# Attention with normalised q and k, then a SiLU feed-forward, on one Trainium2 core: every second product of w_in is summed in a score tile

## The chip, the core and the metric

The program runs on one core of one Trainium2 chip. A core has TensorE (matmuls, PE in the profile), VectorE (DVE), ScalarE (ACT), GpSimd (POOL) and SyncE (SP, which here only issues transfers). They run beside each other, each taking its own instructions in order, and wait for each other by semaphores. Matmuls write to PSUM, which has eight banks of 512 floats in each of 128 partitions; here VectorE and ScalarE read it. The metric is the device time of one execution in microseconds (us), lower is better.

## The reference

Attention for 8 batches of 12 heads, 448 rows, 64 columns each, and then a feed-forward part on the 3584 rows of 768 columns that come out:

```python
q_n, k_n = (rmsnorm(q, g_q), rmsnorm(k, g_k))
scores = scale * np.matmul(q_n, k_n.transpose(0, 1, 3, 2))
attn = softmax(scores)          # exp(scores - max) / (sum + 1e-9)
x = np.matmul(attn, v)          # then (B,H,S,D) -> (B*S, H*D)
h = x @ w_in                    # 768 x 2048
out = (h * (1.0 / (1.0 + np.exp(-h)))) @ w_out      # 2048 x 768
```

All is float32.

## The kernel before

**Attention in visits.** The 96 heads are worked in 24 visits (c = 0 to 23) of four heads. `visit(c)` issues the score matmuls (L712), the exps that empty them (L717, ScalarE), and the weighted sums over v (`weigh`, L749) of this visit and the end of the last one. The sums of the weights are added up on VectorE (`add`, L763). In `between(c)` the next visit's q and k are prepared and `sum_up` (L783) sums the weights over keys with matmuls; two reciprocals (L792, VectorE) read that result, and they are what `divide` needs in the next visit. Up to visit 10, q and k are transposed for the next visit by matmuls: `transpose_q` (L629, emptied by ScalarE, L633) before the first half of `between`, `transpose_k` (L647, emptied by ScalarE, L649) before its second half. From visit 11 on VectorE transposes instead (`flip`, L658), with no PSUM. The squares for the norms are taken by ScalarE and summed by VectorE (L467, L468).

**Products of w_in as filler.** The feed-forward part takes two batches (six visits) at a time. x @ w_in is done with Strassen's scheme in the form with seven products (class `Seven`): for each of eight blocks m of w_in, seven products of three matmul steps each (`HW` = 3), each step a 128x128 by 128x448 matmul. That makes 168 steps for two batches. They are put between the visits of the next six as filler: `fill` is called twice in each `between`, once for each half, and takes steps from the generator until what is due is used up. `filler["due"]` is counted in columns, and `S` = 448 columns are one step. A half holds 13 steps in visits 6 to 11 and 14 in visits 12 to 23 (two blocks of the first two batches are begun earlier, in visits 3 to 5, with 2.4 steps a half). The products of the last two batches come after the visits, in a stage of their own.

Beside the steps, `fill` deals out other work to the queues: the adds, the unpacking and sums of w_in (`weights_in`), the squares for later visits. `prompt` work, the reciprocals above all, is issued at the start of a half and after every third step. When a product has ended, the next thing its generator does is to issue the instruction that empties it: ScalarE's copy for products 1 and 5 (L907, L917), VectorE's add for the others (L857).

**PSUM.** Three pools share the eight banks during the visits. `ps_mm` holds two tiles "mm" of one bank: all products of w_in, and `sum_up` up to visit 4. In `ps`, the tile "sc" has two buffers of two banks each: scores, transposes, `sum_up` from visit 5 on, and one small product in `scale`. "av0" and "av1" take a bank each. After the visits `ps` is closed, and `ps_alone` holds six banks for what follows. A tile's buffer can be written again when all readers of its former tile are done; a matmul that begins the new tile waits for that. The function `bank` (L879) gives a product its place: a tile "mm" during the visits, later one of eight in turn.

The order of all instructions is written out by hand (`manual_schedule`); each engine follows the order of the calls.

Of the kernel before, what the change touches and what calls it, by code (L numbers as in the profile page):

```python
# [11 lines left out]
F32 = mybir.dt.float32  # L12
# [15 lines left out]
BANK = 512  # L28
# [162 lines left out]
def kernel(  # L191
# [246 lines left out]
    with tc.If(taken > 0) as cond:  # L438
        with tc.manual_schedule():
            bounded(**arm())  # L440
# [95 lines left out]
def bounded(  # L536
# [3 lines left out]
    P, D, R, J, S = z.P, z.D, z.R, z.J, z.S  # L540
# [5 lines left out]
    ps = others.enter_context(tc.tile_pool(name="ps", bufs=1, space=bass.MemoryType.PSUM))  # L546
# [14 lines left out]
    work = mem.tile([P, 16 * S + z.NK], F32, name="work")  # L561
# [22 lines left out]
    n = 2 * room.COLS  # L584
# [81 lines left out]
    n = z.NK // z.Q  # L666
# [100 lines left out]
    def sum_up(c):  # L767
# [4 lines left out]
        n = D // 2  # L772
        early = c < GROUP
        t = bank(S) if c < GROUP - 1 else ps.tile([P, 2, BANK], F32, name="sc", bufs=2)[:, 0, 0:S]
        terms = [(0, lambda: weights(c, 0))]
        if early:
# [97 lines left out]
        minus(b21, t2, t4)  # L874

    ps_alone = None
    turns = dict(next=0)

    def bank(n):  # L879
        turn = turns["next"] = (turns["next"] + 1) % 4  # L880
        if ps_alone is None or turn == 0:
            return ps_mm.tile([P, BANK], F32, name="mm")[:, 0:n]
        return ps_alone.tile([P, BANK], F32, name="alone")[:, 0:n]

    class Seven:
# [10 lines left out]
        def product(self, name):  # L896
            t, ends = bank(self.n), (self.steps[0], self.steps[-1])
            for s in self.steps:
                nc.tensor.matmul(  # L899
                    t, self.left(name, s), self.right(name, s), start=s == ends[0], stop=s == ends[1]  # L900
                )
                if not (self.prompt and s == ends[1]):
                    yield self.n
            return t
# [217 lines left out]
    aside = [a[:, ts(t, z.HALF)] for t in range(2)]  # L1122
# [72 lines left out]
    def deep(name, out, more, following, then=lambda t, h: None):  # L1195
# [6 lines left out]
        def product(of):  # L1202
            t = bank(QUARTER)
            for i in ORDER:
                x, y = of_seven(of, a, deep_right(name, i))
                nc.tensor.matmul(t, x[:, i], y, start=i == ORDER[0], stop=i == ORDER[-1])  # L1206
            return t
# [114 lines left out]
        fetch(q + 1, 0, 1)  # L1322


    filler = dict(work=iter(()), due=0.0, share=0.0)

    def begin(work, columns, parts):
        finish()
        filler.update(work=work, due=0.0, share=columns / parts)
# [197 lines left out]
    for c in range(NC):  # L1527
# [4 lines left out]
    ps_alone = ctx.enter_context(  # L1532
        tc.tile_pool(name="ps_alone", bufs=6, space=bass.MemoryType.PSUM)
    )
# [221 lines left out]
```

## Time and profile before

| | |
|---|---|
| Time, median of 3 runs | 1331.36 us (1330.54 to 1336.35) |
| The profiled execution's own time | 1330.28 us |
| Its span, first to last instruction | 1328.5 us |
| TensorE busy | 1298.6 us (98%) |
| VectorE, ScalarE, GpSimd busy | 949.4, 505.7, 362.0 us |
| Mean granted TensorE clock | 0.998 |

In this profile the first 133 us hold visits 0 to 5, the stretch from 133 to 746 us visits 6 to 23 with products of w_in between them, and the rest the last products of w_in and the products with w_out. A float32 matmul is done in two passes, so a step of a product is two rows of MATMUL and a product of three steps is six. Rows of the timeline give the start, the length from the first start to the last end of equal instructions that follow each other, engine, line, operation, the tiles written and read, and in square brackets the idle time before and what ended it. In the view of the waits a line reads: who waits, for whom, us in total, times, the longest.

### The profile page before, as it was taken

What the parts mean: (1) busy time and instruction counts of PE and PEld (TensorE: products, weight loads), DVE (VectorE), ACT (ScalarE), POOL (GpSimd) and SP (SyncE); (2) the same over time, 40 slices, a digit from 0 to 9 for tenths busy, and PEclk for the clock granted to TensorE, in tenths of its full rate; (3) what the DMA queues carried; (4) which work ended last, traced back from release to release, by engine and by line L of the source; (5) the groups of instructions that cost most, each with busy time, mean ns of one, the idle gap of its engine ahead of it and who ended that gap; (6) DMA issues with size and microseconds to landing.
All of it is one profiled execution on the core that took longest, in us unless ns stands there. A gap on an engine that the chain in (4) does not pass through costs nothing.

```text
span 1328.5 us, 19796 instructions
## 1 busy us (share of the span) xinstructions
PE 1298.6 (98%) x7193; PEld 829.5 (62%) x7193; DVE 949.4 (71%) x1629; ACT 505.7 (38%) x886; POOL 362.0 (27%) x230
## 2 busy tenths in 40 slices
PE   8998999999999999999999999999999999999998
PEld 4343444444444444344444455558999999999998
DVE  6888777775855555754554686688978787878785
ACT  7867566645455555455545244410000000001000
POOL 6766444353234333342330144410000000000000
PEclk9999999999999999999999999999999999999999
DMA  9665337234344444344421357512323232332311
GB/s 239 163 178 139 91 90 208 80 88 95 86 116 93 97 98 113 89 94 107 95 67 46 119 174 263 166 66 76 100 76 100 77 104 82 99 107 69 128 48 39
DMA packets 249439, 144.94 MB, mean 109 GB/s; under 512 B 184292, under 2 KB 233220, under 8 KB 249332
## 3 DMA queue, kind: packets, MB, share of 16 engines
q1 hardware_dynamic: 248672, 142.42, 38.2%
q8 instruction: 59, 0.97, 0.3%
q0 software_dynamic: 352, 0.96, 0.2%
q14 instruction: 48, 0.39, 0.1%
q10 hardware_dynamic: 308, 0.20, 0.1%
HBM read 93.98 MB, written 41.29 MB: 102 GB/s over the span
## 4 chain that ended last, share of the span: by engine, by line
PE 83%; DVE 7%; ACT 4%; issue 2%; DMA 2%; POOL 1%; SPq 0%; ACTq 0%; DVEq 0%; POOLq 0%
PE mm L899 24%; PE alone L1206 22%; PE av L749 8%; PE sc L712 8%; PE mm L1206 8%; PE alone L899 7%; PE alone L1243 2%; DVE work L763 2%; PE sc L783 1%; DVE sums_x L854 1%; PE mm L1243 1%; ACT stage L1037 1%; ACT work L717 1%; DMA rows<-in_v_dram 1%; ACT L1037 1%
## 5 line engine op out<-in xcount | busy, mean ns | idle before, releaser
L899 PE MATMUL mm<-x,W 128*128 128x448 f32 x612 | 246.6, 546 | 4.6 <-DVE parts L857 2.1
L717 ACT ACTIVATE work<-sc,rms 128x448 f32<-128x448 f32 x324 | 184.7, 633 | 67.4 <-PE sc L712 62.8
L899 PE MATMUL mm<-sums_x,W 128*128 128x448 f32 x480 | 195.9, 547 | 5.5 <-DVE stage L857 3.8
L899 PEld LDWEIGHTS mm<-x,W 128*128 128x128 f32 x612 | 112.3, 190 | 131.2 <-issue 104.7
L712 PE MATMUL sc<-work 64*64 64x448 f32 x1344 | 164.3, 543 | 1.8 <-ACT work L717 1.5
L763 DVE TENSOR_TENSOR work<-work 128x896 f32<-128x896 f32 (+1 forms) x114 | 123.8, 1117 | 53.5 <-PE av L749 52.9
L749 PE MATMUL av<-work,rows 64*64 64x448 f32 x1296 | 153.4, 541 | 4.1 <-DMA rows<-in_v_dram 2.0
L899 PEld LDWEIGHTS mm<-sums_x,W 128*128 128x128 f32 x480 | 90.1, 191 | 101.0 <-issue 86.0
L496 POOL TENSOR_TENSOR rms<-rms,minus_half 128x14 f32<-128x14 f32 (+4 forms) x43 | 106.3, 2474 | 158.9 <-DVE rms L492 149.4
L523 POOL DMA_DIRECT2D out_dram<-x x2 | 1.2, 594 | 443.3 <-DVE x L857 443.3
L1206 PE MATMUL alone<-W,rows 128*128 128x192 f32 x610 | 113.0, 326 | 0.0
L749 PEld LDWEIGHTS av<-work,rows 64*64 64x64 f32 x1296 | 57.9, 132 | 75.8 <-issue 35.2
L1206 PEld LDWEIGHTS alone<-W,rows 128*128 128x128 f32 x610 | 101.5, 190 | 0.0
L712 PEld LDWEIGHTS sc<-work 64*64 64x64 f32 x1344 | 53.4, 132 | 73.0 <-ACT work L717 27.9
L919 POOL TENSOR_TENSOR parts<-parts,stage 128x448 f32<-128x448 f32 x31 | 42.0, 1356 | 148.5 <-DVE parts L857 148.1
L688 POOL TENSOR_TENSOR rms<-rms,minus_half 128x28 f32<-128x28 f32 x12 | 57.5, 4794 | 61.3 <-DVE rms L685 61.3
L1206 PE MATMUL alone<-W,work 128*128 128x192 f32 x382 | 72.2, 326 | 0.0
L1037 ACT ACTIVATE stage<-stage 128x896 f32<-128x896 f32 x63 | 57.3, 945 | 23.3 <-DVE stage L857 22.5
L468 DVE TENSOR_REDUCE rms<-rows 128x8 f32<-128x512 f32 (+2 forms) x56 | 35.8, 640 | 40.3 <-ACT rows L467 38.8
L1216 ACT COPY rows<-alone 128x192 f32<-128x192 f32 x33 | 10.5, 318 | 142.1 <-PE alone L1206 78.4
L1206 PEld LDWEIGHTS alone<-W,work 128*128 128x128 f32 x382 | 63.8, 190 | 0.0
L792 DVE RECIPROCAL work<-sc 128x224 f32<-128x224 f32 x38 | 58.6, 1546 | 5.4 <-PE sc L783 5.2
(250 smaller groups left out, 2112.6 us busy)
## 6 DMA issues: line engine op xcount, KB each, us to landing
hidden<-stage SPq DMA_DIRECT2D x63, 448.0 KB, 3.1
work<-hidden SPq DMA_DIRECT2D x21, 1024.0 KB, 5.2
rows<-in_moe_w_out_dram SPq DMA_DIRECT2D x32, 384.0 KB, 3.6
W<-in_moe_w_in_dram SPq DMA_DIRECT2D x22, 512.0 KB, 5.4
work<-work SPq DMA_DIRECT2D x141, 56.0 KB, 2.0
x<-hidden SPq DMA_DIRECT2D x7, 1024.0 KB, 5.5
rows<-in_q_dram SPq DMA_DIRECT2D x96, 56.0 KB, 2.2
rows<-in_k_dram SPq DMA_DIRECT2D x96, 56.0 KB, 2.2
```

The lines of the kernel that those rows point to most:

```text
L496: nc.gpsimd.tensor_tensor(out=t, in0=t, in1=half, op=ALU.pow)
L688: nc.gpsimd.tensor_tensor(out=f, in0=f, in1=minus_half.to_broadcast([P, n]), op=ALU.pow)
L712: nc.tensor.matmul(two[ds(half * D, D), h, 0:S], keys[rows, ts(half, D)], qT[rows, pair, :], start=True, stop=True,)
L717: nc.scalar.activation(eleft[:, h] if j == LEFT else weights(c, j)[:, i, h], two[:, h, 0:S], AF.Exp, scale=norm.column(c, i, h, j),)
L749: nc.tensor.matmul(sums[i][ds(h * D, D), :], v, w, start=(j == 0 and step == 1), stop=(j == LEFT - 1 and step == 1),)
L763: nc.vector.tensor_tensor(out=total, in0=total, in1=more, op=ALU.add)
L792: nc.vector.reciprocal(out=r[0][:, rows], in_=t[:, rows])
L899: nc.tensor.matmul(t, self.left(name, s), self.right(name, s), start=s == ends[0], stop=s == ends[1])
L919: nc.gpsimd.tensor_tensor(out=u2, in0=u2, in1=p5, op=ALU.add)
L1037: nc.scalar.activation(t, t, AF.Silu)
L1206: nc.tensor.matmul(t, x[:, i], y, start=i == ORDER[0], stop=i == ORDER[-1])
L1243: nc.tensor.matmul(o, a[:, 2 * i + m, t], right_one(name, i)[:, m], start=n == 0, stop=n == len(steps) - 1,)
```

## The change

`bank` gets a second kind of place during the visits. When a product begins, more than five steps are still due in this half, and the product before it did not get such a place, it is summed in the first bank of a tile "sc" instead of a tile "mm". Otherwise it gets "mm" as before. `turns["aside"]` remembers which the last product had. The dictionary `filler` is defined earlier, since `bank` now reads it; outside `fill` its due is zero or below. Nothing else is changed: the same matmuls in the same order, emptied by the same instructions.

```diff
     ps_alone = None
-    turns = dict(next=0)
+    turns = dict(next=0, aside=False)
+    filler = dict(work=iter(()), due=0.0, share=0.0)
 
     def bank(n):
         turn = turns["next"] = (turns["next"] + 1) % 4
+        if ps_alone is None and filler["due"] > 5 * S and not turns["aside"]:
+            turns["aside"] = True
+            return ps.tile([P, 2, BANK], F32, name="sc", bufs=2)[:, 0, 0:n]
+        turns["aside"] = False
         if ps_alone is None or turn == 0:
             return ps_mm.tile([P, BANK], F32, name="mm")[:, 0:n]
         return ps_alone.tile([P, BANK], F32, name="alone")[:, 0:n]
...
-
-    filler = dict(work=iter(()), due=0.0, share=0.0)
```

## The prediction

> **What bounds the kernel now.** I read the busy shares and the chain first.
>
> ```profile
> PE 1298.6 (98%) x7193; PEld 829.5 (62%) x7193; DVE 949.4 (71%) x1629; ACT 505.7 (38%) x886; POOL 362.0 (27%) x230
> PE 83%; DVE 7%; ACT 4%; issue 2%; DMA 2%; POOL 1%; SPq 0%; ACTq 0%; DVEq 0%; POOLq 0%
> ```
>
> TensorE is the bound, so an edit that adds no work to it is worth what TensorE waits. The waits by pair come next (us in total, times, longest).
>
> ```profile
> PE mm L899 <- DVE stage L857: 5.4, 4, 1.9
> PE mm L899 <- DVE parts L857: 3.0, 6, 0.9
> PE mm L899 <- DVE sums_x L854: 0.6, 1, 0.6
> PE mm L899 <- ACT stage L917: 0.6, 1, 0.6
> ```
>
> Products of w_in (L899) wait 9.6 us in all for other engines, 9.0 us of it for instructions that empty an mm place. So the prize is small: under 1% of 1328.5 us. What one wait is like shows in the timeline of visit 12, when VectorE has a queue.
>
> ```profile
> 345.73 0.91 PE L899 MATMUL mm<-sums_x,W 128*128 128x448 f32 x2
> 348.55 1.40 PE L899 MATMUL mm<-sums_x,W 128*128 128x448 f32 x3 [1.91 <-DVE stage L857]
> ...
> 345.91 2.05 DVE L763 TENSOR_TENSOR work<-work 128x896 f32<-128x896 f32 x2
> 347.88 0.62 DVE L857 TENSOR_TENSOR stage<-mm,stage 128x448 f32<-128x448 f32 x1
> ```
>
> A pass is shown 0.54 long, but passes start 0.37 apart (two rows take 0.91), so a product of six passes takes 2.25 us. The last pass before the wait began at 0.91-0.54 after 345.73, 346.10; the next at 348.55, 2.45 later instead of 0.37. After the wait, three passes take 1.40: two spacings of 0.43 instead of 0.37. A wait thus costs its idle time plus 0.16 plus 0.10. Last, the granted clock (third figure from the end: 1.00, then 0.51) around the twin of this wait, in visit 18:
>
> ```profile
> 551.40:554.80 3.40, 1.52 (x5) 0.47 (x3) 3.40 (x5) 0.00 (x0) 0.00 (x0) 1.00 0.31 51
> 554.80:558.30 3.50, 3.50 (x5) 1.64 (x6) 3.16 (x4) 0.00 (x0) 0.00 (x0) 0.51 0.69 124
> ...
> 554.71 4.22 PE L899 MATMUL mm<-sums_x,W 128*128 128x448 f32 x6 [1.88 <-DVE stage L857]
> ```
>
> After 1.88 us idle the clock is halved for 3.4 us; six passes take 4.22 instead of 2.42.
>
> **What is removed.** In visits 6 to 23 a half holds 13 or 14 steps. By the rule "due over five steps", its first product of those with six to come goes to a score tile, the next to mm, the third again to a score tile if six are left: two per half, mostly. An mm place is then written again two products later than now in the middle of a half, so a product may be emptied some 2.3 us later without a wait. None of the waits above is much longer than that, so all for an mm place go.
> - Listed waits: 9.0, less 0.7 of the four "stage" waits (at 96 us, in visit 4, where no half holds six steps), is 8.3 us in ten waits; with 10 x 0.26 that is **10.9**. The 0.6 for sums_x is for data and stays.
> - Starts held up by 0.06 to 0.3 us, too short for that view (about a dozen in the spacing of the passes, some of them for data): by estimate **2.5** with their 0.10 each.
> - The halved clock: 4.22-2.42 = 1.8, less the 0.10 counted above: **1.7**.
> Removed: 15.1 us.
>
> **What is added.** No engine gets an instruction: same matmuls, same evacuations, other addresses. The moved definition of filler costs nothing. What comes is waits for score tiles, which have their own readers. In visits 6 to 10 the keys are transposed into one (L647) just before the second half, then sum_up takes the other, so the first product of the half falls on the tile of the keys, and waits for ScalarE's copy (L649). The profile has both rows, for visits 7 and 10:
>
> ```profile
> 177.87 0.93 PE L647 MATMUL sc<-ident,rows 128*128 128x128 f32 x7
> 179.61 2.52 PE L899 MATMUL mm<-sums_x,W 128*128 128x448 f32 x6
> ...
> 180.03 0.99 ACT L649 ACTIVATE work<-sc,gains 128x896 f32<-128x896 f32 x1
> ...
> 284.08 2.52 PE L899 MATMUL mm<-x,W 128*128 128x448 f32 x6
> ...
> 283.38 0.67 DVE L468 TENSOR_REDUCE rms<-rows 128x8 f32<-128x512 f32 x1
> ...
> 284.52 0.99 ACT L649 ACTIVATE work<-sc,gains 128x896 f32<-128x896 f32 x1
> ```
>
> The copy is late because ScalarE stands behind a square (L467) that waits for VectorE's sum (L468).
> - Visit 7: copy ends 181.02, product starts 179.61: 1.4 + 0.10. Visit 8: the copy (215.17, 0.99 long) ends 216.16, the product starts 214.68: 1.5 + 0.10.
> - Visit 10: 285.51 against 284.08, 1.4; but the 0.86 idle at 279.97 before it is gone, with its 0.26, and VectorE's row at 283.38 stands behind sums of weights without a gap, so it doesn't come earlier: 1.4 + 1.1 + 0.1 = 2.6.
> - Visits 6 and 9: the copies end at 146.49 and 250.03, the products start 147.87 and 250.37: nothing. In the first half of visit 9 the exps end 237.69, the product starts 237.23: 0.5 + 0.1.
> Together **6.4**. Behind a product that waits stand the whole half on TensorE and, on VectorE, only its own evacuation; the keys' copy is needed in the next visit alone.
> The third product of a second half takes the tile of sum_up, which two reciprocals read:
>
> ```profile
> 320.78 1.54 DVE L792 RECIPROCAL work<-sc 128x224 f32<-128x224 f32 x1
> ...
> 321.77 3.17 PE L899 MATMUL mm<-x,W 128*128 128x448 f32 x8
> ```
>
> The second ends at 322.32, the product starts as the fifth of these passes at 323.28: 0.95 spare, as in most visits from 11 on (0.5 to 2.2). I cost it at nothing; the slow rival lifts that cover. From both sides, the score waits cost 0 (the copies come as in visits 6 and 9) to 2.6 in each of five visits, 13; the three rows decide for 6.4.
>
> **What is late next.** In visit 12 TensorE arrives 2.2 us earlier, but VectorE does not: sum_up (352.51) needs an add that ends at 351.14, so of the new start at 350.3 some 0.8 is waited again; in visit 13 the scores catch up with the exps, which start at 366.27 behind Silu and a table load, 0.7. Visit 18 likewise: 0.5 + 0.4. Given back: **2.4**.
>
> **Sum.** -15.1 + 6.4 + 2.4 = -6.3 against the profiled execution's 1330.28 (span 1328.5 and 1.8 around it). That execution lies 1.1 below the median of 1331.36. The clock term I halve: of the two like waits (1.91 and 1.88) only one drew the half clock, and the new 2.6 us in visit 10 may draw it. That leaves about -5.3, 1325.0 from the profile and 1326.1 from the median: I take **1325.5**.
>
> **The skill against the trace.** Row first: two like waits of 1.9 us, one followed by 3.4 us of half clock. The Trainium skill, "TensorE: Matmul & The Clock Gate", Part 1, says the clock falls after at least one idle window of about 3.4 us; by that no wait here, old or new, would touch it, and the sum would be -4.6 instead of -6.3. The row decides, halved. The same page (HAM oscillation) speaks against the change: in one kernel double-buffered PSUM gave no further gain (126.6 to 125.5). By it the time would stay at 1330; the rows of L857 show that here part of the waiting is for the place.
>
> **The rivals.**
> - *No score wait (faster):* the copies come early enough, or the product gets the other tile. -15.1 + 2.4 = -12.7: **1317.6**. For it: visits 6 and 9. Against: the rows of 7, 8 and 10, and the other tile is read even longer (182.4 and on).
> - *The gain is given back:* VectorE and ScalarE set when the next visit can run, as in visits 12 and 13 in every visit. For it: the scores wait 1.5 us for exps already (L712 for L717, four times). Then only about half the clock term is won: **1329.5**. Against: VectorE is busy 122 of the 206 us from 339 to 545, and its group L763 sat idle 53 us until matmuls (L749), so in most visits it waits for TensorE and not the other way.
> - *Slower, by one mechanism:* TensorE no longer waits for VectorE, reaches sum_up's tile 1.55 (one reciprocal) earlier against it, and waits in its place. 1.55 - 0.95 + 0.26 = 0.9 in sixteen halves is 14: 1324 + 14 = **1338**. It decides from 0.4 us in each. Against: each half shifts only by its own removed wait, 0.1 to 0.6 us in most.
>
> **How the numbers follow.** A measurement can tell about 0.5%, 6.7 us, from no change: 1324.7 to 1338.0. Forecast 0.62 (its own range 1322 to 1329; a third of it under 1324.7), no score wait 0.12, given back 0.19, slower 0.07. Faster: 0.20 + 0.12 = 0.32; slower 0.07; same 0.42 + 0.19 = 0.61. Range 1320 to 1332, which leaves out most of the first and last rival.
>
> **What would show it.** Right: no wait of mm for L857 over 0.3 us; new waits of L899 for L649 in visits 7, 8 and 10 (1.4 to 2.6 us), one for L717 in visit 9; clock 1.00 at 555 us, but perhaps a dip at 287. VectorE, ScalarE and POOL keep their busy times (949, 506, 362). Wrong: waits of L899 for L792 (the slow rival), more waits of L712 for L717 at the start of visits (given back), or L649 early.

## The result, and the profile after

The changed kernel takes 1325.32 us (median of 7 runs, 1322.46 to 1327.29) against 1331.36 us (7 runs, 1329.52 to 1336.35): a ratio of 0.9948, 95% interval 0.9932 to 0.9964. Its profiled execution took 1327.29 us, the longest of the seven, with a span of 1325.5 us at a mean granted clock of 0.998. In the changed kernel the lines behind `bank` stand five lower: the products are L904, the copies of products 1 and 5 are L912 and L922.

Busy shares and chain of the changed kernel:

```profile
PE 1296.1 (98%) x7193; PEld 830.4 (63%) x7193; DVE 949.0 (72%) x1629; ACT 505.7 (38%) x886; POOL 361.4 (27%) x230
...
PE 85%; DVE 6%; ACT 5%; DMA 2%; issue 2%; POOL 0%; SPq 0%; ACTq 0%; DVEq 0%; POOLq 0%
```

No engine has more or less to do than before. What has changed is whom TensorE waits for. The waits by pair (us in total, times, longest):

```profile
PE sc L904 <- ACT work L649: 6.0, 3, 2.6
...
PE mm L904 <- DVE stage L857: 0.7, 1, 0.7
PE sc L904 <- DVE sums_x L854: 0.6, 1, 0.6
PE sc L783 <- DVE work L763: 0.6, 1, 0.6
...
PE sc L783 <- DVE stage L857: 0.5, 1, 0.5
...
PE sc L904 <- ACT work L717: 0.4, 1, 0.4
```

The waits of mm for L857 and L917 have gone from 9.0 to 0.7 us; the one that is left is that in visit 4, where no half holds six steps. In their place products in score tiles wait 6.0 us for ScalarE's copy of the keys. The timeline of visit 12, where TensorE waited 1.91 us before:

```profile
346.75 2.04 PE L904 MATMUL mm<-x,W 128*128 128x448 f32 x5
348.63 2.42 PE L904 MATMUL sc<-sums_x,W 128*128 128x448 f32 x6
350.89 2.42 PE L904 MATMUL mm<-sums_x,W 128*128 128x448 f32 x6
...
350.32 2.05 DVE L763 TENSOR_TENSOR work<-work 128x896 f32<-128x896 f32 x2
352.29 0.62 DVE L857 TENSOR_TENSOR stage<-mm,stage 128x448 f32<-128x448 f32 x1
```

VectorE still begins to empty the first of these products late: it ends at 348.79 and its add (L857) starts at 352.29, behind two adds (L763) of 2.05 us. But the products after it have places of their own, and the three rows on TensorE follow each other at the spacing of 0.37 us, with no idle time in brackets.

**Where the time went.** Both traces hold the same 7193 matmuls in the same order. So I subtracted, matmul by matmul, the interval from one start to the next before from that after, and summed the differences. Before 133 us they sum to +0.7 us (waits for loads, which differ from run to run: -0.9 in the other run), and after 746 us to 0.0. Between, in us:

| where the interval lies | predicted | profile after | changed kernel run again |
|---|---|---|---|
| product waits and short starts removed, with the half clock at 555 us | -15.1 | -16.0 | -16.0 |
| visit 7, product behind `sum_up` | +1.5 | +1.45 | +1.44 |
| visit 8, first product begun in the second half | +1.6 | +2.79 | +1.60 |
| visit 9, first half | +0.6 | +0.51 | +0.51 |
| visit 10: product +2.02, `sum_up` +0.55 | +2.6 | +2.57 | +2.57 |
| half clock at 289 us | perhaps | +1.7 | none |
| given back in later visits | +2.4 | +3.0 | +3.0 |
| sum, from the sums of the intervals | -6.3 | -3.9 | -6.8 |

The last column is the run of the same kernel that is told of below. The removed row is the sum over all product intervals less the rows that follow it; single entries may be off by 0.2. The predicted column is that of the prediction's sum before its clock term was halved.

### The profile page after: what moved, and what is told of

Same layout as the page of the kernel before. It is cut to its first block, busy times and chain, and to the rows that moved or that the text cites. A ratio compares the mean times of both kernels' runs of the same rounds, so it can differ in the third digit from the quotient of the medians.

```text
span 1325.5 us, 19832 instructions
## 1 busy us (share of the span) xinstructions
PE 1296.1 (98%) x7193; PEld 830.4 (63%) x7193; DVE 949.0 (72%) x1629; ACT 505.7 (38%) x886; POOL 361.4 (27%) x230
## 4 chain that ended last, share of the span: by engine, by line
PE 85%; DVE 6%; ACT 5%; DMA 2%; issue 2%; POOL 0%; SPq 0%; ACTq 0%; DVEq 0%; POOLq 0%
PE alone L1211 22%; PE mm L904 16%; PE sc L904 10%; PE av L749 8%; PE sc L712 8%; PE mm L1211 8%; PE alone L904 7%; PE alone L1248 2%; DVE work L763 1%; ACT work L717 1%; PE sc L783 1%; DVE sums_x L854 1%; PE mm L1248 1%; PE mm L783 1%; ACT stage L1042 1%
## 5 line engine op out<-in xcount | busy, mean ns | idle before, releaser
L717 ACT ACTIVATE work<-sc,rms 128x448 f32<-128x448 f32 x324 | 184.5, 633 | 65.5 <-PE sc L712 62.4
L763 DVE TENSOR_TENSOR work<-work 128x896 f32<-128x896 f32 (+1 forms) x114 | 123.8, 1118 | 54.2 <-PE av L749 53.6
L904 PE MATMUL mm<-x,W 128*128 128x448 f32 x354 | 145.8, 543 | 0.7 <-DVE stage L857 0.7
L904 PE MATMUL mm<-sums_x,W 128*128 128x448 f32 x330 | 135.9, 543 | 0.0
L904 PE MATMUL sc<-x,W 128*128 128x448 f32 x258 | 106.7, 550 | 4.6 <-ACT work L649 4.6
L904 PEld LDWEIGHTS mm<-x,W 128*128 128x128 f32 x354 | 65.8, 190 | 69.9 <-issue 67.0
L904 PEld LDWEIGHTS mm<-sums_x,W 128*128 128x128 f32 x330 | 62.0, 191 | 65.3 <-issue 63.4
L904 PEld LDWEIGHTS sc<-x,W 128*128 128x128 f32 x258 | 48.5, 191 | 56.8 <-issue 47.2
L468 DVE TENSOR_REDUCE rms<-rows 128x8 f32<-128x512 f32 (+2 forms) x56 | 35.8, 640 | 39.9 <-ACT rows L467 38.3
```

The lines of the kernel that those rows point to most:

```text
L468: nc.vector.tensor_reduce(out=out, in_=t.rearrange("p (n d) -> p n d", n=n), axis=AX.X, op=ALU.add)
L717: nc.scalar.activation(eleft[:, h] if j == LEFT else weights(c, j)[:, i, h], two[:, h, 0:S], AF.Exp, scale=norm.column(c, i, h, j),)
L763: nc.vector.tensor_tensor(out=total, in0=total, in1=more, op=ALU.add)
L904: nc.tensor.matmul(t, self.left(name, s), self.right(name, s), start=s == ends[0], stop=s == ends[1])
```

## The experiments

In the runs that change who gets a score tile, `bank` is told three things by `between`: the visit `c`, the half (0 or 1) and whether this is the first product of the half. The edit in `bank` is always this, and only the line of `allowed` differs:

```diff
     def bank(n):
         turn = turns["next"] = (turns["next"] + 1) % 4
-        if ps_alone is None and filler["due"] > 5 * S and not turns["aside"]:
+        c, half = turns["c"], turns["half"]
+        first, turns["first"] = turns["first"], False
+        allowed = ...
+        if ps_alone is None and filler["due"] > 5 * S and allowed and not turns["aside"]:
```

The edit adds three lines ahead of the products, so in these runs the products are L907 (in the kernel before that was the line of a copy) and the copies of products 1 and 5 are L915 and L925.

My theory was that of the prediction: a third place takes away the waits for VectorE, and five visits pay some of it back because there the first product of the second half gets the tile that ScalarE still reads for the keys. The rivals were that the gain comes from elsewhere or is lost elsewhere (in attention, or in the tile of `sum_up`).

**Score tiles in visits 11 to 23 alone**, `allowed = c >= 11`:

> Score tiles for products in visits 11 to 23 alone. Theory (place waits are saved, and products of visits 7, 8 and 10 pay 6.0 us for the keys' tile in the changed kernel): the three waits for L649 and the dip of the clock behind the third go, the place waits of visits 6 to 10 come back (1.0 + 0.9 + 0.9 + 0.7 and short ones, about 4.5 with their 0.26 each): 1323.5 us, 1 to 2 under the changed kernel. Rival (what is saved is given back elsewhere, the gain is the halved clock of visit 18 alone): 1329 us. Rival (the keys' tile costs nothing in time, since VectorE is late there anyhow): 1327 us, as these visits' savings are lost.

Measured: 1321.84 us, ratio 0.9932 (0.9917 to 0.9946), nearest to the theory's 1323.5. In its trace no product waits for L649, and 4.0 us of waits for an mm place are left.

**Score tiles in visits 6 to 10 alone**, `allowed = c < 11`:

> Score tiles for products in visits 6 to 10 alone. Theory: about 4.5 us of place waits saved, 6.8 us of waits for the keys' tile added, perhaps a dip of the clock: 1332 to 1334 us, no gain or 1 to 2 slower than before. Rival (given back): 1331 us. Rival (keys' tile costs nothing): 1327 us.

Measured: 1334.10 us, ratio 1.0015 (1.0002 to 1.0027). Its waits by pair hold both kinds:

```profile
PE sc L907 <- ACT work L649: 4.8, 3, 2.0
PE mm L907 <- DVE stage L857: 4.5, 3, 1.9
...
PE mm L907 <- DVE parts L857: 1.3, 4, 0.4
```

The two halves of the change have opposite signs. In visits 11 to 23 it is worth 10.0 us (1331.85 to 1321.84), in visits 6 to 10 it costs 2.3 us. The traces, set start by start against the kernel before, say the same: 8.7 us less behind 310 us in the first run, 1.7 of it the half clock at 555 us, and 2.0 us more between 133 and 310 us in the second. The later visits have no transposes in PSUM, and no wait for L649.

**The tile of the keys spared**, `allowed = not (first and half == 1 and c < 11)`: the first product of the second half goes to mm in visits 6 to 10, and the next may go to a score tile.

> As the changed kernel, but in visits 6 to 10 the first product of a second half gets an mm place, so that no product meets the keys' tile before the second product. Theory: the 6.0 us of waits for L649 go (with 0.26 each 6.8) and the dip, 1 to 3 us of place waits come back: 1321.5 us, 4 under the changed kernel. Rival (keys' tile costs nothing, VectorE is late there anyhow): 1325 us.

Measured: 1320.22 us, ratio 0.9910 (0.9894 to 0.9925). No product waits for L649 any more in the list of the waits. In visit 10 the product starts behind `sum_up` without a wait:

```profile
283.60 0.56 PE L783 MATMUL sc<-work,ones 128*32 128x448 f32 x4
284.08 2.52 PE L907 MATMUL mm<-x,W 128*128 128x448 f32 x6
```

**The control: the same product spared in visits 11 to 23**, where no keys stand in the tile, `allowed = not (first and half == 1 and c >= 11)`:

> The same sparing in the second halves of visits 11 to 23, where no keys lie in a score tile: a control with 13 products where the other has 5. Theory: nothing is won, some place waits come back: 1327 us, 1 to 3 over the changed kernel. Rival (fewer products in score tiles are better in themselves): 1322 us.

Measured: 1329.19 us, ratio 0.9980 (0.9967 to 0.9992). So sparing a product gains nothing by itself; it gives back part of what the third place had won. Waits of mm for L857 return, three of them alike, one in each of visits 13, 16 and 19 (0.55 us each against the changed kernel, set start by start); this is the first:

```profile
392.83 3.55 PE L907 MATMUL mm<-sums_x,W 128*128 128x448 f32 x9
396.76 1.77 PE L907 MATMUL mm<-x,W 128*128 128x448 f32 x4 [0.38 <-DVE parts L857]
```

They make 1.7 us. The median lies 4 us above the changed kernel's, and part of the rest goes with the granted clock, which was 0.993 to 0.997 in nine of its twelve executions; at 0.999 the two kernels are 1326.0 and 1323.8 us on the mean of three executions each, 2.2 apart.

**Only visit 10 spared**, `allowed = not (first and half == 1 and c == 10)`:

> As the changed kernel, but the first product of the second half is kept from the keys' tile in visit 10 alone. Theory: its wait of 2.0 us goes with 0.26, and the dip that may follow it: 1322.5 to 1323.5 us. Rival (one wait only moves VectorE's lateness to the next place): 1325 us.

Measured: 1323.57 us, ratio 0.9931 (0.9914 to 0.9948), with two waits for L649, 4.0 us in all (visits 7 and 8). It lies between the changed kernel and the one that spares all five visits, as the wait of visit 10 alone would have it, but its interval overlaps that of the changed kernel. In its profile the wait of visit 8 is 2.65 us long and is followed by a half clock (3.41 us from 217.5).

**The first product of both halves spared in visits 6 to 10**, `allowed = not (first and c < 11)`, which also takes away the wait of visit 9 for the exps:

> In visits 6 to 10 the first product of either half is kept from a score tile. Theory: as with the second halves alone, and the wait for exps in visit 9 (0.2 to 0.5 us) goes too, against some place waits: 1320 us. Rival (fewer products in score tiles cost more place waits): 1322 us.

Measured: 1320.58 us, ratio 0.9914 (0.9897 to 0.9932). The difference to sparing second halves alone can't be told from the times; the term was 0.5 us, and start by start it is 0.6.

**The changed kernel again**, with no edit, on the chip of the last two runs:

> The changed kernel once more, beside the versions that spare the keys' tile: 1325 us. If it comes near 1320 here, the gain of sparing is of the chip and not of the edit.

Measured: 1324.45 us, ratio 0.9945 (0.9929 to 0.9961). Its profile shows three waits for L649 as before, but 4.8 us in place of 6.0, and no half clock behind them. What differs is visit 8. First ScalarE in the profile after:

```profile
215.04 0.53 ACT L922 COPY stage<-mm 128x448 f32<-128x448 f32 x1 [5.42 <-DMA hidden<-stage]
215.47 0.63 ACT L467 ACTIVATE rows<-rows 128x512 f32<-128x512 f32 x1
216.85 0.52 ACT L467 ACTIVATE rows<-rows 128x384 f32<-128x384 f32 x1 [0.75 <-DVE rms L468]
217.28 0.99 ACT L649 ACTIVATE work<-sc,gains 128x896 f32<-128x896 f32 x1
```

and the same copy with TensorE's product in the run again:

```profile
212.28 0.53 ACT L922 COPY stage<-mm 128x448 f32<-128x448 f32 x1 [4.23 <-DMA hidden<-stage]
...
215.56 2.52 PE L904 MATMUL sc<-x,W 128*128 128x448 f32 x6 [1.44 <-ACT work L649]
```

In visit 8 the keys' copy stands behind the copy of a product into `stage`, and that one waits until an earlier store from `stage` to memory has ended: 5.42 us idle in one execution, 4.23 in the other. The 1.19 us between them is the whole difference of the product's waits, 2.63 and 1.44. The copy waited 4.16 us for that store before the change, too.

**Is the square what makes the copy late?** The changed kernel, every product in its place, but the squares and their sums (L467, L468) of visits 6 to 10 dealt out in the second half:

```diff
-        fill(late + weights_in(c, 0) + further[2:])
+        moved = further[2:] if GROUP <= c < LATE - 1 else []
+        fill(late + weights_in(c, 0) + further[2 + len(moved):])
...
-            fill(weights_in(c, 1) + further[:2], prompt)
+            fill(weights_in(c, 1) + moved + further[:2], prompt)
```

(and `weights_in(c, 1) + moved` likewise in the branch for visit 10).

> The changed kernel, but in visits 6 to 10 the squares of the keys for later visits (L467) and their sums (L468) are dealt out in the second half of `between` instead of the first; every product keeps the place it has in the changed kernel. Theory (the copy of the keys L649 is late because ScalarE stands behind a square that waits for VectorE's sum): the waits of the first product of the second half for L649 fall from 4.8 to 6.0 us in three waits to under 1.6, with none in visits 7 and 10; visit 8 may keep one, since there the copy also stands behind a copy for product 1 or 5 that waits 4 to 5 us for a store to `hidden`. Time 1320 to 1322, near that of the kernel that spares the tile of the keys. Rival (the copy is late for another reason, the transposes, the store or POOL): three waits of 1.4 us or more remain, and the time stays at 1324 to 1326. A second rival: the squares in the second half hold up the evacuations of products there, and the waits come back for L857 or for L922.

Measured: 1321.07 us, ratio 0.9924 (0.9911 to 0.9938). TensorE's waits by pair (us in total, times, longest):

```profile
PE sc L904 <- ACT work L649: 1.0, 3, 0.5
```

and the timeline of visit 7, ScalarE's copy and TensorE's product:

```profile
178.04 1.01 ACT L649 ACTIVATE work<-sc,gains 128x896 f32<-128x896 f32 x1 [0.47 <-PE sc L647]
...
179.10 2.52 PE L904 MATMUL sc<-sums_x,W 128*128 128x448 f32 x6 [0.21 <-ACT work L649]
```

ScalarE now waits for the transposes: its copy starts when they are ready, and the product waits 0.21 us, as it does in visit 10. Visit 8 is at 0.54, though the store was waited for 5.10 us there. So the square in front of the copy is the cause in visits 7 and 10, and the store only adds to it in visit 8. What has moved shows up elsewhere: start by start against the run again, the first products of the second halves take 3.8 us less, while scores that wait for exps at 228 us and a weighted sum that waits for VectorE at 262 us cost 1.0 and 1.3.

**Its control**, the same move of the squares in the kernel before:

> The control for the run beside it: the kernel before (every product in mm) with the same squares of visits 6 to 10 moved to the second half. If moving them acts through the tile of the keys alone, this is the time of the kernel before, 1330 to 1333, with the waits of mm for L857 at 7 to 9 us as before. If the moved squares are worth something by themselves (fewer waits of mm for VectorE in first halves), it lies at 1327 to 1329, and only the difference of the two runs can be credited to the copy of the keys.

Measured: 1329.59 us, ratio 0.9992 (0.9982 to 1.0002). The times don't tell this kernel from the kernel before, though the interval leaves room for 2.4 us, and the trace shows that the move is worth something by itself: waits of products for VectorE in visits 6 to 10 lose about 4 us, and the same scores and weighted sum as above wait 2.3 longer, which makes 1.7 us less. (Behind the 1.9 us waits of visits 12 and 18 the clock was halved both times.) Those waits for VectorE are gone in the changed kernel already. So the 3.8 us beside it, which were waits for L649, came through the tile of the keys; the total times alone would not show it.

**Every product with six steps to come to a score tile**, that is without the alternation (`and not turns["aside"]` taken away, `allowed = True`). This drives the slow rival: `sum_up`'s tile is taken one product earlier.

> Without the alternation: every product with six steps to come goes to a score tile. The second product of a second half then meets the tile of sum_up while its reciprocals (L792) still run, which is what the slow rival of the prediction was about. Theory: waits for L792 of 1 to 2 us in most of the 18 visits, 21 us in all: 1346 us, 15 over the time before. Rival (the place hardly matters, the number of places does): 1325 us, as the changed kernel.

Measured: 1342.22 us, ratio 1.0073 (1.0054 to 1.0092), the only version that is clearly slower. Its waits by pair:

```profile
PE sc L907 <- DVE work L792: 7.9, 8, 2.0
PE sc L907 <- ACT work L649: 5.5, 3, 2.1
...
PE sc L907 <- ACT stage L925: 2.5, 4, 0.6
PE sc L907 <- ACT stage L915: 2.5, 4, 0.6
```

The mechanism of the slow rival is real: products wait for the two reciprocals that read `sum_up`. But it hits eight halves, 7.9 us in all, where I had reckoned with 21; in the other halves the reciprocals ended in time.

The best versions are those in which products don't wait for the keys: 1320.2 to 1321.1 us in three forms (the tile spared in second halves or in both, the squares moved), all with a lower time than both kernels, and not to be told apart from each other.

## Why the prediction was right, point by point

- **The time.** 1325.5 was forecast, 1325.3 measured and 1324.5 in the run again. That the first two agree within 0.2 us is luck: single executions of the changed kernel lie between 1322.5 and 1327.5 us, and terms that were up to 1 us off offset each other. The chance went mostly to "within 0.5%". The ratio of 0.9948, 0.9932 to 0.9964, lies on that bound, so the runs don't show on which side of it the kernel is.
- **What is removed: 15.1 forecast, 16.0 found.** The listed waits went by 8.3 us as said. Summed by intervals, each of the ten waits with the pass behind it, they give 10.9, just what the sum had (8.3 and 0.26 for each); the half clock at 555 us is gone, with its 1.7; and the remaining 3.4 came from short starts, for which 2.5 was an estimate. That term was the one too small.
- **What is added: 6.4 forecast, 7.3 in the profile and 6.1 in the run again.** (The four entries of the prediction add up to 6.3, not 6.4.) All four places were named: L649 in visits 7, 8 and 10, L717 in visit 9. In visit 10 the split was not foreseen: 0.55 of the 2.6 us is waited by `sum_up` for an evacuation (L857), and the product waits 2.02.
- **The cause of the late copy** was put down to the square that waits for VectorE's sum. The run that moves the squares shows it for visits 7 and 10. For visit 8 the step "the copy (215.17, 0.99 long) ends 216.16" took the time of one execution as fixed. The row that I passed over is ScalarE's copy for product 5 just ahead of it, which waits for a store: 4.16 us before, 5.42 in the profile after, 4.23 in the run again. The term was 1.6 and came out as 2.8 and 1.6.
- **The half clock.** That the new wait of visit 10 may draw it was said; it did so once (3.41 us from 289.1), and not in the run again. Over the executions, the mean granted clock was 0.9967 in 49 of the kernel before and 0.9980 in 13 of the changed one. One stretch of 3.41 us at half clock is 3.41 x 0.5 / 1326 = 0.0013, just that difference, so by this estimate the change saves about one such stretch on the mean, 1.7 us. The forecast, with the term halved and the new wait allowed for, had kept 0.7 of it. The single profile of the kernel before, at 0.998, stood above the mean of its executions.
- **Given back: 2.4 forecast, 3.0 found.** Visit 12: 0.86 in `sum_up` (0.8 was said). Visit 13: 0.5, the scores less what the weighted sums behind them win (0.7). Visit 18: 0.84 (0.5). Visit 19: 0.14 (0.4). Two places of 0.35 were not seen beforehand, the scores of visit 11 and `sum_up` at 727 us.
- **The rivals.** "No score wait" did not come, but sparing the keys' tile makes most of it true, and 1320.2 is what that gave, where 1317.6 was worked out. "Given back in every visit" is excluded by the visits from 11 on, which keep 10 us by themselves (8.7 in the trace). The slow rival needs one product more in `sum_up`'s tile; the alternation keeps it away, and in the changed kernel no product waits for L792.
- **The Trainium skill** entered in two places. "TensorE: Matmul & The Clock Gate", Part 1, asks for an idle window of about 3.4 us before the clock falls; here it was halved behind an idle time of 1.95 us. The row, not the page's figure, was the one to go by. The same page's remark (HAM oscillation) that a second PSUM buffer gave one kernel nothing further does not carry over: here a third place is worth 0.5%, and 0.9% where no product waits for the keys' tile.

What stays open: whether the half clock follows the rule that the last section reads off the traces; no run was made to test it.

## What to carry to other kernels

A place borrowed from another pool is not free: look up who reads each of its tiles last, and when, at the point where the newcomer asks for it. Here a third place was worth some 16 us, and 9 to 10 of it went into waits, most of which can be read off the timeline before the change; not borrowing the tile in one spot of five visits won 4 us back. When a wait depends on what stands ahead in an engine's queue, read the whole queue up to the instruction, and take a wait for a transfer in it as a span and not as a number.

## What the runs showed of the hardware

**Half clock after short idle times.** The product behind the wait of visit 10 in the timeline of the profile after:

```profile
288.31 4.14 PE L904 MATMUL sc<-x,W 128*128 128x448 f32 x6 [1.95 <-ACT work L649]
```

and the windows of busy time by engine around it:

```profile
285.60:289.00 3.40, 1.45 (x10) 0.49 (x3) 2.78 (x5) 2.14 (x4) 0.77 (x1) 1.00 0.12 28
289.00:292.50 3.50, 3.50 (x6) 1.58 (x5) 2.03 (x2) 3.49 (x4) 2.60 (x5) 0.51 0.60 109
```

The third figure from the end is the granted clock, 0.51 in the second stretch; six passes take 4.14 us, and 2.52 in the run again at full clock. Waits of 1.9 us in visits 12 and 18 were followed by it in five of six cases (kernel before, score tiles in visits 6 to 10, control of the squares), the wait of visit 10, 1.95 us each time, in one of five (profile after, the run again, score tiles in visits 6 to 10, the control of the late products, every product). Each time it cost about 1.7 us.

The traces say more about when it comes. In all twelve, every switch of the granted clock lies a whole number of 3.413 us behind its first rise (in the profile after 83 x 3.413 = 283.3 us, from 5.76 to 289.07). Cut along this grid up to 1300 us, they hold 4511 stretches at full clock, the first two of each trace left out (one trace was halved behind its first, at 54% busy). Behind the 4495 in which matmuls kept TensorE busy for more than 45% the clock was never halved, behind the other 16 it was in 13. In the profile after the wait of visit 10 lay in one stretch, busy for 1.47 of 3.41 us; in the run again the same wait, 283.61 to 285.56, lay across the boundary at 284.33, both stretches were busy for 2.2 us, and the clock stayed full. The rule was read off afterwards and no edit tested it, and it does not tell apart the like waits of the kernel before in visit 12 (44.6%, full clock) and visit 18 (44.9%, halved).

**Most of the scatter between runs goes with the granted clock.** In the control that spares late products, executions at 0.999 took 1326.0 us on the mean and those at 0.993 took 1332.6: 6.6 us for 0.006, near the 0.006 x 1326 = 8.0 that a clock alone would make.
